# Late banks of sums, folds that wait for company, and a traded place: one edit to a planned FNet-and-attention kernel

## The chip, the cores and the metric

The kernel runs on one core of one Trainium2 chip. The metric is the device time of one execution in microseconds (us); smaller is better. The core has a matrix engine, TensorE (PE, with its weight loads shown apart as PEld), VectorE (DVE), ScalarE (ACT), GpSimd (POOL) and SyncE (SP), which here does nothing but issue transfers (DMAs). Each engine works through its own list of instructions in order; semaphores make one wait for another. TensorE writes into PSUM, which is used here as eight banks of 128 x 512 float32.

## The reference, cut to what matters

Two independent sublayers on 2048 tokens of width 448 are computed in float32 and laid side by side in the output (2048 x 896).

```
# A: FNet mixing
a = einsum("bsd,ed->bse", x, dft_hid_re);  b = einsum("bsd,ed->bse", x, dft_hid_im)
y = einsum("ts,bse->bte", dft_seq_re, a) - einsum("ts,bse->bte", dft_seq_im, b)
# B: full softmax attention, 16 heads of 28
qkv = x @ wqkv;  scores = q @ k.T * 28 ** -0.5;  p = softmax(scores, axis=-1)
out = concat_heads(p @ v) @ wo
concatenate([A, B], axis=-1)
```

The inputs of B are scaled up by 8 each, so the scores are large and the maximum has to be taken off before the exponential.

## The kernel before, in words

**Precision.** Most products run in TensorE's fast float32 form (F32R, one pass). An operand is split into a high part (`hi`) and the rest (`lo`), and hi*hi, lo*hi and hi*lo are summed: three products in place of one. Two kinds of product use plain float32 instead: probabilities times V (L736, "PV") and the fold of its partial sums (L878). Both work in column strips of the array that are 32 wide (128*32 in the profile), all others on 128 columns except a small transpose (L718).

**Stage work ("fill").** Q, K, V projections (`project`, `values`, L548), part A's hidden transforms (`hidden`, L548) and its sequence transforms (`sequence`, L663: 1536 products of 448 columns). Each takes its weights as pieces (`Piece`): a DMA into `wraw`, a cast on ACT (`whi`, L517), a subtraction on POOL (`wlo`, L523), three places of each. Fill accumulates in two PSUM banks of its own.

**Attention.** A head's 2048 queries are four chunks of 512; a unit is one chunk of one head, 64 in all, in two lanes.
- A *kept* unit (44; `unit_kept`) makes 16 score products with keys in rows (L809). ACT copies each to SBUF (L416; two score tiles share a place of the pool `kept`, a "pair"), while DVE keeps the running maximum over the tiles in `rm` (L816, L819). Then DVE turns `rm` into one maximum per query, copied to all partitions: transpose (L824), reduce (L826), three small copies (L831), a reduce over those (L836), two small copies (L834), transpose back (L842); ACT copies the result to `mb` (L844). POOL (or DVE, reading the bank) takes it off each pair (L859), ACT takes the exponential (L863), and two groups of eight PV products follow (`pv_group`).
- A *twice* unit (20; `unit_twice`) makes its scores twice: once with queries in rows (L755; DVE reduces the maximum, L759), and, after the maximum has gone through DRAM into two more rows of q, once with keys in rows (L787), which ACT exponentiates straight out of the bank (L791); then PV.

Each unit's PV accumulates in one bank `po`, copied to a place of `ou` (`unit_out`). When all units of a head are through, `out_of` folds them (L878) and sends sums and quotients through DRAM. The output projection (L988) closes the program.

**What sets the order.** Nothing is ordered by hand. `Schedule` plays the engines forward with planned costs and emits, for each engine, the ready task with the smallest key (a due time); a task that needs a place (a bank, a pair, a place of `q` or `ou`) takes it when it is emitted and gives it back when its last user is done. The planner knows that a change of TensorE between the two kinds of float costs time (`PE_TURN`): once in float32 it first looks for another float32 task (`mode` 1). `units`' due times come from `T_ATT`, `T_END` and the `ahead` factors, those of fill from `T_FILL`. The lists that come out are fixed; on the chip each engine follows its list.

**Places before.** Six banks for attention; 19 pairs in `kept`; 4 places of `q`; 5 of `ou`.

Of the kernel before, what the change touches and what calls it, by code (L numbers as in the profile page):

```python
# [24 lines left out]
P = 128  # L25
# [7 lines left out]
NKEPT = 19  # L33
# [32 lines left out]
PE_TURN = 0.33  # L66

# [99 lines left out]
class Task:  # L167
    __slots__ = ("engs", "key", "emit", "lat", "use", "lock", "left", "then", "mode", "n", "dmas", "own", "since")


class Schedule:
# [11 lines left out]
    def add(self, engs, key, emit, deps=(), acq=(), use=(), lat=0.15, lock=(), mode=0, dmas=(), own=0.0):  # L183
        t = Task()
        t.own = own
# [20 lines left out]
    def run(self):  # L206
# [10 lines left out]
        while True:  # L217
            for e in self.ENGINES:
# [8 lines left out]
                while heap:  # L227
# [8 lines left out]
                    if t.since > before or any(not p.can_take(w, before, now) for p, w in wants.items()) or any(  # L236
                            x.lock > now + 1e-9 for x in t.lock):
                        aside.append(item)
                        continue
# [79 lines left out]
def tile_kernel(ctx, tc, xa, wre, wim, wd, xb, wqkv, wo, out):  # L319
# [33 lines left out]
    q_s = new("q", [P, CH], F32R, 4, True)  # L353
# [3 lines left out]
    ou_s = new("ou", [P, CH], F32, 5, True)  # L357
# [63 lines left out]
    T_ATT, T_END, T_FILL, T_OUT = 34.0, 1100.0, 1130.0, 1100.0  # L421
# [6 lines left out]
    for lane, per, ahead, part in ((lane_r, P_R, 1.08, 1.0), (lane_k, P_K, 2.0, 1.0)):  # L428
# [220 lines left out]
    def sequence(part, made):  # L649
        src = wim if part else wre  # L650
        for tt in range(NT):
# [3 lines left out]
            for q in range(4):  # L655
                key = fkey(12, M448)
                w = Piece(lambda tt=tt, q=q: src[tt, :, q * 4:q * 4 + 4, :], key - 12)
# [86 lines left out]
    def unit_twice(u):  # L744
# [34 lines left out]
        for g in range(NT // GV):  # L779
            tiles, es = [], []  # L780
            for kt in range(GV * g, GV * (g + 1)):
                o = bank_s.slot()
                if kt % 2 == 0:
# [5 lines left out]
                    deps=[ld, before.get("rb")], use=[o, p.pair, q, KT[h][kt // 4], po])  # L789
# [6 lines left out]
    def unit_kept(u):  # L796
# [29 lines left out]
        r = dve(key, lambda o=o: nc.vector.tensor_reduce(  # L826
# [3 lines left out]
        def beside(i):  # L830
            return lambda: nc.vector.tensor_copy(pm.t[:32, i * NT:(i + 1) * NT], pm.t[32 * i:32 * i + 32, :NT])  # L831

        def back(n, o=o):
            return lambda: nc.vector.tensor_copy(o.t[n:2 * n, :NT], o.t[:n, :NT])  # L834
        r = [dve(key, beside(i), SMALL, deps=[r], use=[pm]) for i in (1, 2, 3)]
        r = dve(key, lambda o=o: nc.vector.tensor_reduce(  # L836
            o.t[:32, :NT], pm.t[:32, :4 * NT].rearrange("p (i j) -> p j i", i=4), axis=AX.X, op=ALU.min), 0.25,
            deps=r, use=[pm, o])
        for n in (32, 64):
            r = dve(key, back(n), SMALL, deps=[r], use=[o])  # L840

        t = dve(key, lambda o=o: nc.vector.transpose(pm.t, o.t[:, :NT].unsqueeze(2).to_broadcast([P, NT, 32])), 0.64,  # L842
                deps=[r], use=[pm, o])
# [25 lines left out]
    def out_of(us, rd):  # L869
# [9 lines left out]
        m = pe(key, emit, d=0.86, deps=[ou_done[u] for u in us], use=[o, *(OU[u] for u in us)], mode=1)  # L879
# [154 lines left out]
```

## Time and profile before

| | before |
|---|---|
| median of 3 runs | 1154.09 us (1153.95 to 1154.94) |
| the profiled execution's own time | 1154.71 us |
| its span, first to last instruction | 1152.5 us |
| busy: PE / PEld | 1140.0 (99%) / 780.5 (68%) us |
| busy: DVE / ACT / POOL | 988.2 (86%) / 1028.2 (89%) / 905.0 (79%) us |
| mean granted TensorE clock | 0.997 |
| PV products L736, records | 1960 + 88, mean 601 and 594 ns |

How to read it: matmuls are pipelined, so one is listed with some 0.37 to 0.41 us though the next starts 0.2 us later. What a stretch of TensorE costs is therefore read from start to start in the timeline, not from the listed durations. A float32 product shows as two records. In the timeline, rows are "start, length, engine, line, operation, out<-in", instructions of one group merged (x8), with idle time in brackets.

### The profile page before, as it was taken

What the parts mean: (1) busy time and instruction counts of PE and PEld (TensorE: products, weight loads), DVE (VectorE), ACT (ScalarE), POOL (GpSimd) and SP (SyncE); (2) the same over time, 40 slices, a digit from 0 to 9 for tenths busy, and PEclk for the clock granted to TensorE, in tenths of its full rate; (3) what the DMA queues carried; (4) which work ended last, traced back from release to release, by engine and by line L of the source; (5) the groups of instructions that cost most, each with busy time, mean ns of one, the idle gap of its engine ahead of it and who ended that gap; (6) DMA issues with size and microseconds to landing.
All of it is one profiled execution on the core that took longest, in us unless ns stands there. A gap on an engine that the chain in (4) does not pass through costs nothing.

```text
span 1152.5 us, 19482 instructions
## 1 busy us (share of the span) xinstructions
PE 1140.0 (99%) x6110; PEld 780.5 (68%) x6110; DVE 988.2 (86%) x1767; ACT 1028.2 (89%) x1765; POOL 905.0 (79%) x540
## 2 busy tenths in 40 slices
PE   8999999999999999999999999999999999999998
PEld 6976566566676667766767766666666767757577
DVE  6599988899898999999999989989899888899812
ACT  5269999899998999989999999999999899899952
POOL 3038688799798998988988899987998789596660
PEclk9999999899999999999999999999999999999999
DMA  9984344132323232232323232232333333323543
GB/s 266 186 197 144 115 163 131 44 86 76 101 86 101 83 91 68 86 105 91 108 79 102 77 115 67 84 105 96 106 96 94 94 94 105 114 64 95 157 153 122
DMA packets 111880, 125.18 MB, mean 109 GB/s; under 512 B 49369, under 2 KB 63353, under 8 KB 111777
## 3 DMA queue, kind: packets, MB, share of 16 engines
q1 hardware_dynamic: 111776, 123.94, 35.9%
q8 instruction: 48, 0.79, 0.3%
q14 instruction: 56, 0.45, 0.1%
HBM read 90.00 MB, written 33.77 MB: 107 GB/s over the span
## 4 chain that ended last, share of the span: by engine, by line
PE 86%; DVE 6%; ACT 3%; issue 2%; DMA 1%; SPq 0%; DVEq 0%; ACTq 0%
PE bank L663 25%; PE bank L736 19%; PE bank L809 13%; PE bank L548 12%; PE bank L755 6%; PE bank L787 6%; PE bank L988 3%; DVE rm L819 3%; ACT kept L416 1%; PE bank L878 1%; ACT kept L791 1%; DVE mx L759 1%; DMA kept<-wqkv 1%; DMA kept<-xb 1%; ACT kept L863 0%
## 5 line engine op out<-in xcount | busy, mean ns | idle before, releaser
L859 POOL TENSOR_TENSOR kept<-kept,mb 128x1024 f32<-128x1024 f32 x259 | 617.3, 2407 | 68.1 <-ACT mb L844 54.5
L819 DVE TENSOR_TENSOR rm<-bank,rm 128x512 f32<-128x512 f32 x616 | 421.9, 685 | 57.2 <-ACT kept L416 20.9
L416 ACT ACTIVATE kept<-bank 128x512 f32<-128x512 f32 (+1 forms) x673 | 390.9, 642 | 54.0 <-PE bank L809 34.2
L863 ACT ACTIVATE kept<-kept 128x1024 f32<-128x1024 f32 x343 | 370.6, 1118 | 7.8 <-POOL kept L859 5.6
L663 PE MATMUL bank<-big,whi 128*128 128x448 f32 x1024 | 325.8, 368 | 0.0
L523 POOL TENSOR_TENSOR wlo<-wraw,whi 128x512 fp32r<-128x512 f32 (+1 forms) x166 | 204.7, 1236 | 129.2 <-ACT whi L517 71.2
L809 PE MATMUL bank<-q,k 84*128 84x512 f32 x704 | 270.6, 410 | 3.3 <-DVE bank L842 1.4
L736 PE MATMUL bank<-kept,v 128*32 128x512 f32 x1960 | 242.0, 601 | 0.3 <-DVE rm L819 0.3
L759 DVE TENSOR_REDUCE mx<-bank 128x1 f32<-128x512 f32 x320 | 216.3, 681 | 11.1 <-PE bank L755 8.6
L663 PEld LDWEIGHTS bank<-big,whi 128*128 128x128 f32 x1024 | 193.9, 190 | 30.2 <-issue 4.2
L791 ACT ACTIVATE kept<-bank 128x512 f32<-128x512 f32 x294 | 184.1, 650 | 7.6 <-PE bank L787 7.5
L663 PE MATMUL bank<-big,wlo 128*128 128x448 f32 x512 | 188.2, 368 | 0.0
L809 PEld LDWEIGHTS bank<-q,k 84*128 84x128 f32 x704 | 129.4, 188 | 76.1 <-DVE rm L819 11.6
L736 PEld LDWEIGHTS bank<-kept,v 128*32 128x32 f32 x1960 | 56.6, 110 | 123.6 <-issue 112.9
L755 PE MATMUL bank<-k,q 84*128 84x512 f32 x320 | 130.4, 414 | 0.5 <-DVE mx L759 0.2
L787 PE MATMUL bank<-q,k 86*128 86x512 f32 x320 | 127.9, 410 | 0.1
L517 ACT ACTIVATE whi<-wraw 128x512 fp32r<-128x512 f32 x167 | 115.4, 691 | 5.9 <-DMA wraw<-wqkv 2.5
L663 PEld LDWEIGHTS bank<-big,wlo 128*128 128x128 f32 x512 | 97.1, 190 | 12.4
L859 DVE TENSOR_TENSOR kept<-kept,bank 128x1024 f32<-128x1024 f32 x84 | 100.9, 1210 | 4.6 <-ACT mb L844 4.6
L787 PEld LDWEIGHTS bank<-q,k 86*128 86x128 f32 x320 | 59.8, 189 | 35.3 <-issue 6.7
L755 PEld LDWEIGHTS bank<-k,q 84*128 84x128 f32 x320 | 60.3, 189 | 33.7 <-DVE rm L819 8.3
L548 PE MATMUL bank<-wd,whi 128*128 128x448 f32 x256 | 79.2, 368 | 0.1
(82 smaller groups left out, 1065.0 us busy)
## 6 DMA issues: line engine op xcount, KB each, us to landing
wraw<-wre SPq DMA_DIRECT2D x64, 256.0 KB
wraw<-wim SPq DMA_DIRECT2D x64, 256.0 KB
qkd<-wd SPq DMA_DIRECT2D x32, 256.0 KB
wraw<-xa SPq DMA_DIRECT2D x32, 256.0 KB
k<-qkd SPq DMA_DIRECT2D x64, 112.0 KB
q<-qkd SPq DMA_DIRECT2D x64, 112.0 KB
out<-kept SPq DMA_DIRECT2D x31, 224.0 KB
qkd<-kept SPq DMA_DIRECT2D x24, 256.0 KB
```

Of the source, the lines that this page charges most:

```text
L416: nc.scalar.activation(dst, src, AF.Copy)
L523: b = sch.add(e, at, lambda g: eng[g].tensor_tensor(self.lo.t[:, :n], raw.t[:, :n], f32(self.hi.t)[:, :n], op=ALU.subtract), deps=[a], acq ...
L548: nc.tensor.matmul(o.t[:, :cols], w(), x(), start=(i == 0), stop=(i == n - 1))
L663: nc.tensor.matmul(o.t[:, :D], a.t[:, k, :], b[:, q * 4 + k, :], start=(q == 0 and k == 0 and j == 0), stop=(q == 3 and k == 3 and j == 2))
L736: nc.tensor.matmul(o.t[j * VW:(j + 1) * VW, :], VT[h].t[:, kt // 4, j, :], pairs[i // 2].t[:, i % 2, :], start=(kt < 4), stop=(kt >= NT - 4))
L755: m = pe(key, lambda e, o=o, kc=kc, qt=qt: nc.tensor.matmul(o.t, q.t[:KR, qt * P:(qt + 1) * P], KT[h][kc].t[:KR, :], start=True, stop=True ...
L759: ms.append(dve(key - 20, lambda o=o, kc=kc, qt=qt: nc.vector.tensor_reduce(mx.t[:, qt, kc:kc + 1], o.t, axis=AX.X, op=ALU.max), deps=[m], ...
L787: m = pe(key, lambda e, o=o, kt=kt: nc.tensor.matmul(o.t, KT[h][kt // 4].t[:KR + 2, kt % 4 * P:(kt % 4 + 1) * P], q.t[:KR + 2, :], start=T ...
L809: m = pe(key, lambda e, o=o, kt=kt: nc.tensor.matmul(o.t, KT[h][kt // 4].t[:KR, kt % 4 * P:(kt % 4 + 1) * P], q.t[:KR, :], start=True, sto ...
L819: prev = dve(key - 20, lambda o=o: nc.vector.tensor_tensor(rm.t, o.t, rm.t, op=ALU.max), deps=[m, prev], use=[rm, o], lock=[o], own=RAW)
L859: eng[e].tensor_tensor(s.t, s.t, over_pair(pm.t if e == "DVE" else mb.t), op=ALU.add)
L863: es.append(act(key, lambda s=s: nc.scalar.activation(s.t, s.t, AF.Exp, scale=SCALE), 0.96, deps=[sh], use=[s]))
```

## The change

It does six things, all through the planner's inputs.

1. *Banks of sums late.* In `unit_twice` the 16 second score products no longer use `po`, so the bank is taken by the first PV group and not by the first second score.
2. *First bank of the maxima.* In `unit_kept` the bank that the first transpose fills is given back after the reduce. The small copies and the small reduce now stay inside the second bank (columns 64 to 80), and the transpose back writes a third.
3. *Folds wait.* A fold that is ready while TensorE is in the fast form is put off until a PV group is ready too, or 15 planned us have passed (`JOIN`), or nothing else is ready; not in the last 30 us of attention.
4. *Places.* `kept` 20 pairs in place of 19, paid with one place of `q` (4 to 3) and one of `ou` (5 to 4).
5. *Keys.* `T_END`, `T_OUT` 1100 to 1104, `T_FILL` 1130 to 1132; `ahead` 1.08 to 1.07 and 2.0 to 2.06.
6. *Pieces* of `sequence` are due one planned us earlier.

No product is added or taken away.

```diff
-NKEPT = 19
+NKEPT = 20
+JOIN = 15.0
...
+                    if e == "PE" and mode == 0 and t.wait and now - t.since < t.wait and not any(
+                            y[2].mode == 1 and y[2].n not in done for y in heap):
+                        first = first or item
+                        aside.append(item)
+                        continue
...
-    q_s = new("q", [P, CH], F32R, 4, True)
+    q_s = new("q", [P, CH], F32R, 3, True)
-    ou_s = new("ou", [P, CH], F32, 5, True)
+    ou_s = new("ou", [P, CH], F32, 4, True)
...
-    T_ATT, T_END, T_FILL, T_OUT = 34.0, 1100.0, 1130.0, 1100.0
+    T_ATT, T_END, T_FILL, T_OUT = 34.0, 1104.0, 1132.0, 1104.0
-    for lane, per, ahead, part in ((lane_r, P_R, 1.08, 1.0), (lane_k, P_K, 2.0, 1.0)):
+    for lane, per, ahead, part in ((lane_r, P_R, 1.07, 1.0), (lane_k, P_K, 2.06, 1.0)):
...
-                w = Piece(lambda tt=tt, q=q: src[tt, :, q * 4:q * 4 + 4, :], key - 12)
+                w = Piece(lambda tt=tt, q=q: src[tt, :, q * 4:q * 4 + 4, :], key - 13)
...
-                    deps=[ld, before.get("rb")], use=[o, p.pair, q, KT[h][kt // 4], po])
+                    deps=[ld, before.get("rb")], use=[o, p.pair, q, KT[h][kt // 4]])
...
-            return lambda: nc.vector.tensor_copy(o.t[n:2 * n, :NT], o.t[:n, :NT])
+            return lambda: nc.vector.tensor_copy(pm.t[n:2 * n, 4 * NT:5 * NT], pm.t[:n, 4 * NT:5 * NT])
...
-        t = dve(key, lambda o=o: nc.vector.transpose(pm.t, o.t[:, :NT].unsqueeze(2).to_broadcast([P, NT, 32])), 0.64,
-                deps=[r], use=[pm, o])
+        p1, pm = pm, bank_s.slot()
+        t = dve(key, lambda pm=pm: nc.vector.transpose(pm.t, p1.t[:, 4 * NT:5 * NT].unsqueeze(2).to_broadcast([P, NT, 32])), 0.64,
+                deps=[r], use=[pm, p1])
...
-        m = pe(key, emit, d=0.86, deps=[ou_done[u] for u in us], use=[o, *(OU[u] for u in us)], mode=1)
+        m = pe(key, emit, d=0.86, deps=[ou_done[u] for u in us], use=[o, *(OU[u] for u in us)], mode=1,
+               wait=JOIN if key < T_END - 30 else 0.0)
```

The whole list of every engine is reordered, from the first attention units on. Three places follow. Line numbers of the changed kernel are 6 to 8 higher: L736 is L742, L755 L761, L787 L793, L809 L815, L859 L866, L878 L885, L988 L996.

TensorE, the last fold of a head with four units in both programs (`ou` are its four units' sums, `fold` the constant that adds them). Before:

```order
L718 MATMUL bank_231<-ident,nm_220 4x128
L809 MATMUL bank_226<-q_188,k_184 128x512
L809 MATMUL bank_228<-q_188,k_184 128x512
L809 MATMUL bank_230<-q_188,k_184 128x512
L663 MATMUL bank_224<-big,whi_173 128x448
L878 MATMUL bank_227<-ou_215,fold 32x512
L878 MATMUL bank_227<-ou_216,fold 32x512
L878 MATMUL bank_227<-ou_214,fold 32x512
L878 MATMUL bank_227<-ou_213,fold 32x512
L809 MATMUL bank_231<-q_188,k_184 128x512
```

Now:

```order
L742 MATMUL bank_227<-kept_209,v_186 32x512 x2
L742 MATMUL bank_226<-kept_208,v_186 32x512 x2
L742 MATMUL bank_226<-kept_203,v_186 32x512 x2
L742 MATMUL bank_226<-kept_192,v_186 32x512 x2
L742 MATMUL bank_226<-kept_205,v_186 32x512 x2
L885 MATMUL bank_230<-ou_213,fold 32x512
L885 MATMUL bank_230<-ou_215,fold 32x512
L885 MATMUL bank_230<-ou_214,fold 32x512
L885 MATMUL bank_230<-ou_216,fold 32x512
L815 MATMUL bank_228<-q_190,k_185 128x512
```

The fold stood alone between fast products; it now stands behind two PV groups.

DVE, the maxima of the last kept unit (banks by their numbers). Before:

```order
L824 STREAM_TRANSPOSE bank4_228<-rm0_211 128x512
L826 TENSOR_REDUCE bank3_227<-bank4_228 128x16
L831 COPY bank3_227<-bank3_227 32x16 x3
L836 TENSOR_REDUCE bank4_228<-bank3_227 32x16
L834 COPY bank4_228<-bank4_228 32x16
L834 COPY bank4_228<-bank4_228 64x16
L842 STREAM_TRANSPOSE bank3_227<-bank4_228 128x512
```

Now:

```order
L830 STREAM_TRANSPOSE bank7_230<-rm0_211 128x512
L832 TENSOR_REDUCE bank4_227<-bank7_230 128x16
L837 COPY bank4_227<-bank4_227 32x16 x3
L842 TENSOR_REDUCE bank4_227<-bank4_227 32x16
L840 COPY bank4_227<-bank4_227 32x16
L840 COPY bank4_227<-bank4_227 64x16
L849 STREAM_TRANSPOSE bank2_225<-bank4_227 128x512
```

The first bank was in use over all seven rows; it is now in use over two.

TensorE in part A's first hidden transform, ahead of the two PV groups that stand between its third piece of weights (`whi_172`) and its fourth. Before:

```order
L548 MATMUL bank_225<-wd,whi_172 128x448 x2
L809 MATMUL bank_229<-q_191,k_183 128x512
L809 MATMUL bank_226<-q_191,k_183 128x512
L809 MATMUL bank_230<-q_191,k_183 128x512
L755 MATMUL bank_228<-k_180,q_189 128x512
L809 MATMUL bank_231<-q_191,k_183 128x512
L755 MATMUL bank_228<-k_180,q_189 128x512
L755 MATMUL bank_227<-k_180,q_189 128x512
L755 MATMUL bank_228<-k_180,q_189 128x512
L736 MATMUL bank_229<-kept_202,v_187 32x512 x2
```

Now:

```order
L554 MATMUL bank_224<-wd,whi_172 128x448
L761 MATMUL bank_225<-k_180,q_190 128x512
L793 MATMUL bank_229<-q_189,k_180 128x512
L554 MATMUL bank_224<-wd,wlo_175 128x448
L761 MATMUL bank_228<-k_182,q_190 128x512
L554 MATMUL bank_224<-wd,whi_172 128x448 x2
L793 MATMUL bank_230<-q_189,k_180 128x512
L742 MATMUL bank_227<-kept_209,v_187 32x512 x2
```

Before, the third piece was used up and eight score products stood there without fill among them; now products with the third piece stand between the scores up to the PV groups (one more follows behind them).

More of the change, by code (lines that the diff above doesn't have):

```diff
@@ L167 @@
 class Task:
-    __slots__ = ("engs", "key", "emit", "lat", "use", "lock", "left", "then", "mode", "n", "dmas", "own", "since")
+    __slots__ = ("engs", "key", "emit", "lat", "use", "lock", "left", "then", "mode", "n", "dmas", "own", "since", "wait")
 class Schedule:
@@ L181, in __init__, with add @@
         self.now = 0.0
-    def add(self, engs, key, emit, deps=(), acq=(), use=(), lat=0.15, lock=(), mode=0, dmas=(), own=0.0):
+    def add(self, engs, key, emit, deps=(), acq=(), use=(), lat=0.15, lock=(), mode=0, dmas=(), own=0.0, wait=0.0):
         t = Task()
-        t.own = own
+        t.own, t.wait = own, wait
         t.engs, t.key, t.emit, t.lat, t.lock, t.mode = engs, key, emit, lat, lock, mode
@@ L825, in unit_kept, with back @@
         pm = bank_s.slot()
-        r = dve(key, lambda o=o: nc.vector.tensor_reduce(
+        r = dve(key, lambda o=o, pm=pm: nc.vector.tensor_reduce(
             pm.t[:, :NT], o.t.rearrange("p (j r) -> p j r", r=32), axis=AX.X, op=ALU.max, negate=True), deps=[t], use=[o, pm], own=RAW_S)
         def beside(i):
-            return lambda: nc.vector.tensor_copy(pm.t[:32, i * NT:(i + 1) * NT], pm.t[32 * i:32 * i + 32, :NT])
-        def back(n, o=o):
-            return lambda: nc.vector.tensor_copy(o.t[n:2 * n, :NT], o.t[:n, :NT])
+            return lambda pm=pm: nc.vector.tensor_copy(pm.t[:32, i * NT:(i + 1) * NT], pm.t[32 * i:32 * i + 32, :NT])
+        def back(n, pm=pm):
+            return lambda: nc.vector.tensor_copy(pm.t[n:2 * n, 4 * NT:5 * NT], pm.t[:n, 4 * NT:5 * NT])
         r = [dve(key, beside(i), SMALL, deps=[r], use=[pm]) for i in (1, 2, 3)]
-        r = dve(key, lambda o=o: nc.vector.tensor_reduce(
-            o.t[:32, :NT], pm.t[:32, :4 * NT].rearrange("p (i j) -> p j i", i=4), axis=AX.X, op=ALU.min), 0.25,
-            deps=r, use=[pm, o])
+        r = dve(key, lambda p1=pm: nc.vector.tensor_reduce(
+            p1.t[:32, 4 * NT:5 * NT], p1.t[:32, :4 * NT].rearrange("p (i j) -> p j i", i=4), axis=AX.X, op=ALU.min), 0.25,
+            deps=r, use=[pm])
         for n in (32, 64):
-            r = dve(key, back(n), SMALL, deps=[r], use=[o])
-        t = dve(key, lambda o=o: nc.vector.transpose(pm.t, o.t[:, :NT].unsqueeze(2).to_broadcast([P, NT, 32])), 0.64,
-                deps=[r], use=[pm, o])
+            r = dve(key, back(n), SMALL, deps=[r], use=[pm])
+        p1, pm = pm, bank_s.slot()
+        t = dve(key, lambda pm=pm: nc.vector.transpose(pm.t, p1.t[:, 4 * NT:5 * NT].unsqueeze(2).to_broadcast([P, NT, 32])), 0.64,
+                deps=[r], use=[pm, p1])
         ld = act(key, lambda: nc.scalar.activation(mb.t, pm.t, AF.Copy), deps=[t], use=[pm, mb], lock=[pm])
```

## The prediction

> **What bounds the kernel now.** I read the page first (busy time, the forty slices, the chain that ended last), then the timeline of TensorE start to start, then the windows around its gaps.
>
> ```profile
> PE 1140.0 (99%) x6110; PEld 780.5 (68%) x6110; DVE 988.2 (86%) x1767; ACT 1028.2 (89%) x1765; POOL 905.0 (79%) x540
> PE   8999999999999999999999999999999999999998
> PE 86%; DVE 6%; ACT 3%; issue 2%; DMA 1%; SPq 0%; DVEq 0%; ACTq 0%
> ```
>
> TensorE has work in every slice and the chain runs through it for 86%. So the end moves by what leaves TensorE's list, and by the stalls in it; what the other four engines gain or lose counts only where TensorE waits. All 6110 records are products that the change keeps. What can change is the cost of going between the two kinds of product, and the stalls.
>
> **The price of a turn.** A visit to the float32 products, one PV group, then a visit of two groups, then a fold alone:
>
> ```profile
> 403.61 0.39 PE L809 MATMUL bank<-q,k 84*128 84x512 f32 x1
> 403.84 0.37 PE L663 MATMUL bank<-big,whi 128*128 128x448 f32 x1
> 404.05 0.37 PE L663 MATMUL bank<-big,wlo 128*128 128x448 f32 x1
> ...
> 405.29 0.39 PE L755 MATMUL bank<-k,q 84*128 84x512 f32 x1
> 405.61 1.06 PE L736 MATMUL bank<-kept,v 128*32 128x512 f32 x8
> ...
> 407.46 0.73 PE L787 MATMUL bank<-q,k 86*128 86x512 f32 x2
> 408.04 0.37 PE L663 MATMUL bank<-big,whi 128*128 128x448 f32 x1
> ```
>
> ```profile
> 398.43 0.62 PE L736 MATMUL bank<-lent,v 128*32 128x512 f32 x2
> ...
> 402.00 0.73 PE L809 MATMUL bank<-q,k 84*128 84x512 f32 x2
> ```
>
> ```profile
> 223.18 0.36 PE L548 MATMUL bank<-wd,whi 128*128 128x448 f32 x1
> 223.47 1.07 PE L878 MATMUL bank<-ou,fold 128*32 128x512 f32 x8
> 224.47 0.51 PE L809 MATMUL bank<-q,k 84*128 84x512 f32 x1
> 224.81 0.40 PE L787 MATMUL bank<-q,k 86*128 86x512 f32 x1
> ```
>
> An ordinary score product takes 403.84 - 403.61 = 0.23 us from start to start, one of 448 columns 404.05 - 403.84 = 0.21. More closely, the 66 products of the last row but one quoted below take (13.66 - 0.37) / 65 = 0.205, and 512/448 of that is 0.235 for the scores. Three losses make up a turn. Going in: 405.61 - 405.29 = 0.32 where 0.235 is usual, 0.09 lost (the fold: 0.29 for 0.205, the same). Coming out: two groups in one visit take 402.00 - 398.43 = 3.57, one takes 407.46 - 405.61 = 1.85; so a group is worth 1.72 and 0.13 is lost. Then the first fast product behind it: two took 408.04 - 407.46 = 0.58 for 0.47, 0.11 lost (behind the fold 0.34 for 0.235, 0.10). The sum is **0.33 us a turn**, whatever stands in the visit.
>
> **The change, part by part.**
>
> *Turns.* Counting visits over the two lists of TensorE: 111 before, 97 now. Folds that make a visit alone fall from 7 to 2, which is the waiting fold's work (3 of the change). Visits with PV fall from 104 to 95 for the same 128 groups: visits of a single group from 83 to 66, of two from 18 to 25, of three from 3 to 4. That comes from the replanning as a whole. 14 x 0.33 = **4.6 us** off a list that has no cover of its own: it goes off the end unless a stall takes it back.
>
> *The largest stall.* TensorE's longest gap after the start-up is the place of the third order piece.
>
> ```profile
> 202.99 0.39 PE L809 MATMUL bank<-q,k 84*128 84x512 f32 x1
> 203.94 1.10 PE L809 MATMUL bank<-q,k 84*128 84x512 f32 x2 [0.56 <-DVE rm L819]
> 206.26 0.79 PE L809 MATMUL bank<-q,k 84*128 84x512 f32 x1 [0.63 <-DVE rm L819]
> 209.16 1.08 PE L736 MATMUL bank<-kept,v 128*32 128x512 f32 x4
> ```
>
> ```profile
> 203.80 0.68 DVE L759 TENSOR_REDUCE mx<-bank 128x1 f32<-128x512 f32 x1
> 204.40 0.68 DVE L819 TENSOR_TENSOR rm<-bank,rm 128x512 f32<-128x512 f32 x1
> ...
> 193.04 14.19 POOL L859 TENSOR_TENSOR kept<-kept,mb 128x1024 f32<-128x1024 f32 x6
> 207.18 1.01 POOL L523 TENSOR_TENSOR wlo<-wraw,whi 128x384 fp32r<-128x384 f32 x1
> ```
>
> ```profile
> 180.00:202.00 22.00, 22.00 (x123) 14.70 (x122) 20.65 (x38) 21.40 (x38) 18.91 (x13) 1.00 0.44 140
> 202.00:210.00 8.00, 6.44 (x18) 2.73 (x20) 7.71 (x14) 7.87 (x14) 7.36 (x6) 0.74 0.10 28
> ```
>
> ```profile
> 209.23 5.36 PE bank L736 x32
> 398.50 3.57 PE bank L736 x32
> ```
>
> POOL subtracts six pairs in a row (14.19 us) and the next `wlo` is ready only at 208.2. Out of fill, TensorE has eight score products, each of which needs a bank that DVE empties at 0.60 us apiece (204.40 - 203.80). From 202.99 to 209.16 they take 6.17 us; eight at 0.235 are 1.88 and the turn's 0.09 belongs to the turn: 4.2 lost. In the same window the granted clock (the third number from the end) is 0.74, 1.00 in the window ahead, and the two PV groups behind take 5.36 where two take 3.57 at 398.50: 1.8 more. So this stall is worth **6.0 us**. The Trainium skill (TensorE: Matmul & The Clock Gate, Part 1) says that the clock is halved once a window of 3.4 us sees too little activity. By that rule any stall that trips it costs half a window, 1.7 us, on top of itself, which the 1.8 us above bears out; the no-change rival below would then end at 1155.4.
>
> In the new list the eight products in a row are gone, with fill between the scores up to the PV groups. But the run of six subtractions on POOL is still there between the third and the fourth piece, so I can't exclude that TensorE runs dry in front of the fourth. Bounds: 6.0 us gained, or nothing. I take half, **3.0 us**.
>
> *Banks.* The late `po` leaves one of six banks free while the first eight second scores of each of 20 units go through; the early return of the first bank spares it from the reduce to the end of the transpose back:
>
> ```profile
> 74.56 0.60 DVE L831 COPY bank<-bank 32x16 f32<-32x16 f32 x3
> 75.19 0.22 DVE L836 TENSOR_REDUCE bank<-bank 32x16 f32<-32x64 f32 x1
> 75.88 0.73 DVE L842 STREAM_TRANSPOSE bank<-bank 128x512 f32<-128x512 f32 x1
> ...
> 75.52 0.40 PE L548 MATMUL bank<-big,wlo 128*128 128x512 f32 x1
> 76.66 1.08 PE L809 MATMUL bank<-q,k 84*128 84x512 f32 x2 [0.74 <-DVE bank L842]
> ...
> PE bank L809 <- DVE bank L842: 1.4, 2, 0.7
> ```
>
> Here TensorE waited for just that bank; the preceding product started at 75.52, so 0.90 us was lost (76.66 - 75.52 - 0.235). A third bank is now wanted for the transpose back, so a wait there can be new too. By this row the 44 units could gain up to 0.90 each at a place like this, but TensorE's waits on L842 are 2 in all (1.4 us), so the bounds are 1.4 gained and, with a new wait as long at two places, 1.4 lost. I take nothing: the planner has already spent the spare banks on the denser order counted above. The small reduce now reads and writes one bank; the copies L831 do that in 0.20 each, the reduce took 0.22 between two banks. Even at twice that, 44 x 0.22 = 10 us lie in DVE's idle 164.
>
> *Work that changes engine.* In the lists DVE has 15 more copies of banks (65 to 80, 0.60 us each) and 4 fewer subtractions of a pair (85 to 81), ACT 15 fewer copies, POOL 4 more subtractions (2.4 us each). DVE gains some 4 us of work and POOL 10, under 164 and 248 us idle. The cover is gone only in stretches like the one at 203.
>
> *One place of `q` less.* This is the edit that speaks against the change. I added up TensorE's products, at their distances above, between the last one that reads a place of `q` and the first of the place's next unit. Before: 24 us in the median, under 6 us in 3 cases of 60. Now: 7.0 us in the median, under 6 us in 19 of 61, never under 5.0. A new load must fit into that.
>
> ```profile
> 36.05 0.46 SPq L690 DMA_DIRECT2D q<-qkd  x1
> 36.56 0.42 SPq L691 DMA_DIRECT2D q<-qkd  x1
> ...
> 40.32 0.40 PE L755 MATMUL bank<-k,q 84*128 84x512 f32 x1
> ```
>
> The two transfers of a load were issued from 36.05 and the product that reads them started at 40.32 without a wait: at most 4.27 us. The last reader's length, 0.4, comes ahead of it. That makes 4.7 against 5.0, so a load fits where SP is free, by the loosest bound. SP isn't always free:
>
> ```profile
> SPq L516 <- POOL wlo L523: 160.0, 81, 10.3
> ```
>
> SP takes its list in order, and stands 81 times, up to 10.3 us, in front of a load of weights whose place POOL hasn't freed; a load of `q` behind it waits as well, and behind that TensorE's next score, and everything in its list. Bounds: nothing, or a microsecond in each of the 19 cases, 19 us. I take **1.0 us**, since the planned order knows of SP's waits and the surplus is only what the plan has wrong. [...]
>
> *The end.* The keys put attention's end later against fill. The last fold's results must come back before the last 44 products:
>
> ```profile
> 1135.23 13.66 PE L988 MATMUL bank<-wd,k 128*128 128x448 f32 x66
> 1135.27 1.55 DVE L412 TENSOR_TENSOR k<-kept,k 128x256 fp32r<-128x256 f32 x4
> ```
>
> The last chunk's products begin 22 x 0.205 behind 1135.23, at 1139.7; their operands were ready at 1136.8: 2.9 us to spare. In the new list, TensorE has 27.1 us of work between the last fold and those products, where the old list has 28.2. So 1.8 us are left: nothing lost; if the chain were 3 us slower, 1.2 us would be.
>
> *Start.* TensorE's list is the same over its first 73 rows, into the first score products, so the start-up gaps stay.
>
> **The sum.** 1152.5 - 4.6 - 3.0 + 1.0 = 1145.9 us of span. The median of the runs lies 1.6 above the profiled span (1154.09; the profiled execution itself took 1154.71, 2.2 above). So **1147.5 us**, 0.57% less.
>
> **Rivals.**
>
> *Slower: loads of q late.* One mechanism: SP stands behind a weight load, the load of q is issued late, and TensorE's list stops at that unit's first score. For it: 19 gaps under 6 us where there were 3. Against: 4.7 us is the loosest bound. From 0.40 us in each of the 19 cases it eats the 7.6 of both gains, from 0.52 the kernel is slower by 0.2%; at 0.6 the time is 1154.1 - 4.6 - 3.0 + 11.4 = 1157.9. Chance 0.11.
>
> *No change: the stalls move.* TensorE runs dry in front of the fourth piece as before (the 3.0 is not gained) and one stall more of the size of the one at 203, without the clock's share (4.2), appears: 1154.1 - 4.6 + 4.2 = 1153.7. For it: DVE and ACT are at 86 and 89%, and a reordered list meets new places. Chance 0.16.
>
> *Faster than I say.* All of the stall at 203 goes and q costs nothing: 1154.1 - 4.6 - 6.0 = 1143.5; with the waits on L842 too, 1142.1. Chance 0.15.
>
> *The change does nothing that it says* is excluded by the lists: 97 visits are 97.
>
> **Chances and range.** My forecast, turns gained and stalls no worse, has 0.58. A measurement of this kernel tells about 0.2% from no change, 2.3 us: faster is below 1151.8, slower above 1156.4. The forecast (0.58, all but 0.03 of it below 1151.8) and the faster rival (0.15) make 0.70 for faster; of the no-change rival 0.13 and the 0.03 give 0.16 for the same; the late loads and 0.03 of the moved stalls, 0.14 for slower. The range 1142 to 1154 takes in the faster rival's end and all of the no-change rival's point, and leaves out the slower one and a tail; the forecast's own range is 1144.5 to 1150.5.
>
> **What would show it.** Right: two-group visits more often, 14 fewer turns at the same 0.33; at about 195 to 215 us no half clock, and L736 x32 at 3.57; no wait of TensorE behind L690 or L691. Wrong: gaps in front of a unit's first score with a load of q as the releaser; a window with the clock under 1.00; a stall of TensorE in front of the fourth hidden piece; or turns that cost other than 0.33 when the groups stand closer.

## The result and the profile after

The changed kernel takes 1146.94 us (median of 6, 1145.6 to 1149.28), the kernel before, beside it, 1155.2 us (median of 6, 1153.95 to 1156.85): a ratio of 0.993, 95% interval 0.9917 to 0.9943. The forecast was 1147.5. The profiled execution of the changed kernel took 1145.6, the fastest of its six; its span is 1143.7. What the traces below split up is one execution of each kernel, and executions of one list differ (the six here by 3.7 us), so a term of a microsecond or two is not sure.

The same lines of the page as before, now of the changed kernel (busy time of each engine; TensorE's slices; shares of the chain that ended last):

```profile
PE 1133.0 (99%) x6110; PEld 782.5 (68%) x6110; DVE 988.6 (86%) x1777; ACT 1024.7 (90%) x1750; POOL 914.5 (80%) x545
PE   9999999999999999999999999999999999999998
PE 90%; DVE 4%; ACT 3%; issue 2%; DMA 1%; SPq 0%; DVEq 0%; ACTq 0%
```

TensorE has the same 6110 records and the chain now runs through it for 90% instead of 86%. Line numbers have moved: L736, L809, L819, L842 and L859 of the kernel before are L742, L815, L825, L849 and L866 now. Where the 8.7 us of span went is read from the distances of TensorE's starts. In every trace I added them up: each product at the distance that its form has inside its own kind (0.205 or 0.235, a PV group 1.717, a fold 0.859), each visit to the float32 products at 0.33, and the rest is called stalls. The products alone come to 1088.1 us in every list here (42 small transposes are in that; with their median distances it would be some 2 us less, and the stalls of every row 2 us more, alike), the first product starts at 1.4, and what lies behind the last start is called the end.

| kernel | median | span | visits | turns | stalls before 30 us | stalls behind 30 us | end |
|---|---|---|---|---|---|---|---|
| before | 1155.2 | 1152.5 | 111 | 36.7 | 5.2 | 17.1 | 4.0 |
| after | 1146.9 | 1143.7 | 97 | 32.1 | 4.0 | 13.9 | 4.2 |

Turns give 4.6, stalls behind 30 us 3.2, stalls before 30 us 1.2, the end takes 0.3 back: 8.7 us of span. The 1.2 before 30 us is no part of the change: the list of TensorE is the same there, and over the nine traces of whole kernels (these two and the seven below without added products) this term lies between 4.0 and 5.9. It can be seen on one product that both lists have at the same place, before and now:

```profile
30.05 0.39 PE L548 MATMUL bank<-big,wlo 128*128 128x512 f32 x1
```

```profile
28.83 0.39 PE L554 MATMUL bank<-big,wlo 128*128 128x512 f32 x1
```

The 3.2 hides two large terms of opposite sign. The stall at 203 us is gone. Windows of the changed kernel, the first the one that the prediction shows of the kernel before (stretch, its length, then busy time of PE, PEld, DVE, ACT, POOL, then the granted clock, share of DMA, GB/s):

```profile
202.00:210.00 8.00, 8.00 (x53) 4.36 (x52) 7.69 (x18) 8.00 (x14) 7.19 (x6) 1.00 0.20 53
...
1055.00:1063.00 8.00, 7.70 (x49) 4.05 (x37) 8.00 (x11) 8.00 (x13) 7.86 (x7) 1.00 0.39 123
1063.00:1071.00 8.00, 6.61 (x29) 3.81 (x31) 7.31 (x12) 8.00 (x14) 4.15 (x4) 0.79 0.39 131
```

TensorE's timeline at the first of them (start, duration, engine, line), then POOL's:

```profile
205.09 0.57 PE L554 MATMUL bank<-wd,whi 128*128 128x448 f32 x2
205.50 0.40 PE L793 MATMUL bank<-q,k 86*128 86x512 f32 x1
205.83 3.64 PE L742 MATMUL bank<-kept,v 128*32 128x512 f32 x32
209.41 0.74 PE L815 MATMUL bank<-q,k 84*128 84x512 f32 x2
```

```profile
194.43 11.87 POOL L866 TENSOR_TENSOR kept<-kept,mb 128x1024 f32<-128x1024 f32 x5
206.26 1.01 POOL L529 TENSOR_TENSOR wlo<-wraw,whi 128x384 fp32r<-128x384 f32 x1
```

TensorE is busy for all of the 8 us where it had 6.44, the clock is 1.00 where it was 0.74, and the 32 records of PV take 209.41 - 205.83 = 3.58 where they took 5.36. POOL still has a run of subtractions (five in 11.87 us; it was six in 14.19), and the next `wlo` is only 1 us earlier. What changed is what TensorE has until then: fill up to 205.5, and behind it two PV groups that start 3.3 us earlier than they did. They cover the wait for `wlo`.

In its place there is a new stall, near the end of attention. TensorE's timeline, then DVE's ahead of it:

```profile
1062.33 0.36 PE L669 MATMUL bank<-big,wlo 128*128 128x448 f32 x1
1063.67 0.50 PE L815 MATMUL bank<-q,k 84*128 84x512 f32 x1 [0.97 <-DVE rm L825]
1064.80 0.50 PE L793 MATMUL bank<-q,k 86*128 86x512 f32 x1 [0.63 <-DVE kept L866]
1065.40 0.79 PE L815 MATMUL bank<-q,k 84*128 84x512 f32 x1
1065.98 0.57 PE L669 MATMUL bank<-big,whi 128*128 128x448 f32 x1
```

```profile
1053.69 1.21 DVE L866 TENSOR_TENSOR kept<-kept,bank 128x1024 f32<-128x1024 f32 x1
1054.82 0.69 DVE L825 TENSOR_TENSOR rm<-bank,rm 128x512 f32<-128x512 f32 x1
1055.42 1.21 DVE L866 TENSOR_TENSOR kept<-kept,bank 128x1024 f32<-128x1024 f32 x1
```

DVE has subtractions of the last units (L866) between its maxima (L825): by these rows a score bank comes free every 1055.42 - 1053.69 = 1.73 us, where maxima alone free one in 0.60. By the windows above DVE is busy 8.00 of 8 from 1055 to 1063; then scores wait for banks, the clock falls to 0.79 (a window with the clock under 1.00 was one of the prediction's signs of being wrong), and in all 4.5 us are lost between 1060 and 1070. So the stalls behind 30 us are -5.9 at 203, +4.5 at 1063 and -1.8 in all the other places.

### The profile page after: what moved, and what is told of

Same layout as the page of the kernel before. It is cut to its first block, busy times and chain, and to the rows that moved or that the text cites. A ratio compares the mean times of both kernels' runs of the same rounds, so it can differ in the third digit from the quotient of the medians.

```text
span 1143.7 us, 19466 instructions
## 1 busy us (share of the span) xinstructions
PE 1133.0 (99%) x6110; PEld 782.5 (68%) x6110; DVE 988.6 (86%) x1777; ACT 1024.7 (90%) x1750; POOL 914.5 (80%) x545
## 4 chain that ended last, share of the span: by engine, by line
PE 90%; DVE 4%; ACT 3%; issue 2%; DMA 1%; SPq 0%; DVEq 0%; ACTq 0%
PE bank L669 26%; PE bank L742 19%; PE bank L815 14%; PE bank L554 13%; PE bank L761 7%; PE bank L793 6%; PE bank L996 3%; PE bank L885 1%; DVE rm L825 1%; ACT kept L422 1%; ACT kept L797 1%; ACT kept L870 1%; DMA kept<-wqkv 1%; DMA kept<-xb 0%; DVE mx L765 0%
## 5 line engine op out<-in xcount | busy, mean ns | idle before, releaser
L866 POOL TENSOR_TENSOR kept<-kept,mb 128x1024 f32<-128x1024 f32 x259 | 619.0, 2413 | 73.4 <-ACT mb L851 65.4
L825 DVE TENSOR_TENSOR rm<-bank,rm 128x512 f32<-128x512 f32 x616 | 421.5, 684 | 43.2 <-ACT kept L422 13.4
L870 ACT ACTIVATE kept<-kept 128x1024 f32<-128x1024 f32 x340 | 369.5, 1130 | 8.6 <-POOL kept L866 4.6
L529 POOL TENSOR_TENSOR wlo<-wraw,whi 128x512 fp32r<-128x512 f32 (+1 forms) x166 | 205.5, 1241 | 105.1 <-ACT whi L523 76.4
L815 PE MATMUL bank<-q,k 84*128 84x512 f32 x704 | 266.3, 411 | 2.5 <-DVE rm L825 1.3
L742 PE MATMUL bank<-kept,v 128*32 128x512 f32 x1960 | 240.5, 596 | 0.0
L797 ACT ACTIVATE kept<-bank 128x512 f32<-128x512 f32 x300 | 192.6, 671 | 4.2 <-PE bank L793 4.1
L815 PEld LDWEIGHTS bank<-q,k 84*128 84x128 f32 x704 | 129.5, 188 | 79.3 <-DVE rm L825 19.3
L742 PEld LDWEIGHTS bank<-kept,v 128*32 128x32 f32 x1960 | 57.8, 109 | 123.8 <-issue 107.0
L793 PE MATMUL bank<-q,k 86*128 86x512 f32 x320 | 128.1, 406 | 1.0 <-DVE kept L866 0.6
L761 PE MATMUL bank<-k,q 84*128 84x512 f32 x320 | 127.8, 407 | 0.3 <-ACT kept L870 0.2
L866 DVE TENSOR_TENSOR kept<-kept,bank 128x1024 f32<-128x1024 f32 x81 | 97.6, 1211 | 5.9 <-ACT mb L851 5.4
L761 PEld LDWEIGHTS bank<-k,q 84*128 84x128 f32 x320 | 60.0, 188 | 30.8 <-DVE rm L825 4.1
L793 PEld LDWEIGHTS bank<-q,k 86*128 86x128 f32 x320 | 60.2, 189 | 24.5 <-DVE rm L825 5.3
```

Of the source, the lines that this page charges most:

```text
L529: b = sch.add(e, at, lambda g: eng[g].tensor_tensor(self.lo.t[:, :n], raw.t[:, :n], f32(self.hi.t)[:, :n], op=ALU.subtract), deps=[a], acq ...
L742: nc.tensor.matmul(o.t[j * VW:(j + 1) * VW, :], VT[h].t[:, kt // 4, j, :], pairs[i // 2].t[:, i % 2, :], start=(kt < 4), stop=(kt >= NT - 4))
L761: m = pe(key, lambda e, o=o, kc=kc, qt=qt: nc.tensor.matmul(o.t, q.t[:KR, qt * P:(qt + 1) * P], KT[h][kc].t[:KR, :], start=True, stop=True ...
L793: m = pe(key, lambda e, o=o, kt=kt: nc.tensor.matmul(o.t, KT[h][kt // 4].t[:KR + 2, kt % 4 * P:(kt % 4 + 1) * P], q.t[:KR + 2, :], start=T ...
L815: m = pe(key, lambda e, o=o, kt=kt: nc.tensor.matmul(o.t, KT[h][kt // 4].t[:KR, kt % 4 * P:(kt % 4 + 1) * P], q.t[:KR, :], start=True, sto ...
L825: prev = dve(key - 20, lambda o=o: nc.vector.tensor_tensor(rm.t, o.t, rm.t, op=ALU.max), deps=[m, prev], use=[rm, o], lock=[o], own=RAW)
```

## Experiments

Ratios are to the kernel before, run on the same chip, with 95% intervals. The five kernels of the next part were run once each and have no interval.

### What a turn costs

The prediction read 0.33 us a turn out of neighbouring starts. Here turns are put in. In the middle of each of the 128 PV groups, behind the fourth of its eight products, stand two more. They add zeros to the group's bank, so the sums stay what they are. `identr` is the constant `ident` held as a float32r tile; the columns 96 to 99 of its first 96 rows are zeros.

```diff
...
                                  start=(kt < 4), stop=(kt >= NT - 4))
+                if i == 3:
+                    for _ in range(2):
+                        nc.tensor.matmul(o.t[:, :4], identr[:96, :], identr[:96, 96:100], start=False, stop=False)
```

The other four have another line in the place of the last: float32 over 128 columns (`ident[:96, :]` and `ident[:96, 96:100]`), fast in a strip of 32 (`o.t[:VW, :4]`, `identr[:96, :VW]`), float32 in a strip (the same of `ident`), and fast with 448 columns, one column of zeros read 448 times.

The fast pair over 128 columns:

> The changed kernel with two small fast products (96 rows, 128 columns of a constant, 4 columns of zeros, added to the bank) put into the middle of each of the 128 PV groups: 128 visits more, 225 in all, and 256 small products; the result of each sum is unchanged. Theory (a change there and back costs 0.33 us whatever stands between): 1146.9 + 128 x 0.33 = 1189 us, and the 256 products' own length on top, as the control with the same products of the groups' own kind has it. Rival (what I read as a turn belongs to the score products' operands, not to the change of kind): no more than the control, and 0.1 us or less between a group's halves beside the products.

The float32 pair over 128 columns:

> The same place, two small float32 products over 128 columns of the constant. Theory K (the price belongs to the change between float32 and fast products): no turn, so the control's time. Theory S (it belongs to the change between strips of 32 columns and the full 128): 128 x 0.33 = 42 us above the control, as much as the fast pair.

The fast pair in a strip:

> The same place, two small fast products over a strip of 32 columns. Theory K (change between float32 and fast): 42 us above the control. Theory S (change between strip and full width): the control's time.

The control, float32 in a strip:

> The control: the same place, two small float32 products over a strip of 32 columns, the groups' own kind. Both theories: no turn, 97 visits; 1146.9 us and the 256 products' own length, which the trace gives as the distance of their starts (by the length of a whole strip product, 0.21 us for 512 columns, at most 256 x 0.21 = 55 us).

The fast pair of 448 columns:

> As the fast pair in the middle of each PV group, but the two fast products have 448 columns (all zeros), whose distance of starts the rows give as 0.205 us. Theory (a turn costs 0.33 us, 0.10 of it at the second fast product): a visit of a single group takes 1.854 + 0.33 + 2 x 0.205 = 2.59 us, the whole 1146.9 + 128 x 0.74 = 1241.6 us. Rival (0.19 us, what the pair of 4 columns shows in its steps out and back in, without a loss at the second product): 2.45 us a visit, 1223 us.

Times: 1195.89, 1226.18, 1177.16, 1157.01 and 1230.97 us. In the times, part of the added work is hidden in stalls that were there anyway, so the visits tell more. For the visits of one PV group that stand complete in the trace (55 in each), the medians of the distances between starts, in ns. A group has four sets of records, four strips each, that start 7 apart; the row of a set gives the distance from its last record to what comes next. The pair stands between the second set and the third:

| | whole visit | set 1 | set 2 | inside the pair | pair to set 3 | set 3 | set 4, to the score or fill behind |
|---|---|---|---|---|---|---|---|
| after, no pair | 1854 | 433 | 409 | | | 409 | 523 |
| fast, 128 columns | 2305 | 433 | 522 | 133 | 181 | 433 | 522 |
| float32, 128 columns | 2530 | 433 | 523 | 132, 112, 112 | 182 | 433 | 523 |
| fast, strip | 2145 | 433 | 522 | 53 | 101 | 433 | 522 |
| float32, strip | 1963 | 433 | 409 | the pair's records run among the third set's | | | 523 |
| fast, 448 columns | 2570 | 434 | 522 | 293 | 285 | 433 | 522 |

(A float32 product has two records, so a float32 pair has four.)

One visit of the last of these kernels as its timeline shows it (L745 are the strips of PV, L749 the pair):

```profile
408.56 0.36 PE L672 MATMUL bank<-big,whi 128*128 128x448 f32 x1
408.85 1.07 PE L745 MATMUL bank<-kept,v 128*32 128x512 f32 x8
409.85 0.65 PE L749 MATMUL bank<-ident 96*128 96x448 f32 x2
410.43 1.06 PE L745 MATMUL bank<-kept,v 128*32 128x512 f32 x8
411.43 0.50 PE L821 MATMUL bank<-q,k 84*128 84x512 f32 x1
```

The pair of 448 columns makes a visit 0.716 us longer. Two such products are worth 0.410; **0.306 us** is the turn put in. Its parts stand in the steps: out 522 - 409 = 0.113, and 0.024 in the first set behind the return (433 for 409); 293 - 205 = 0.088 at the second fast product; 285 - 205 = 0.080 going back in. That is the 0.13, 0.10 and 0.09 of the prediction, 8% smaller in sum, and near the theory's 2.59 us (2.57), not the rival's 2.45. The time of the whole, 1230.97, is 10.6 under the theory's 1241.6: 128 x 0.716 = 91.6 us were added and 84.0 appeared (85.4 by the spans, 1229.1 for 1143.7). So the stalls became some 6 us shorter; that the other engines used the longer time to catch up is likely, and not shown.

Of the theories on what makes the turn, neither K nor S holds. The strip pair changes only the kind, the wide float32 pair only the width, and both pay the same 0.11 out and 0.02 behind the return as the pair that changes both; the control, which changes neither, pays nothing (409 behind its second set). So a visit ends wherever the next product differs in kind or in width. The Trainium skill (TensorEngine Tiling (Array Packing), Key Properties) says that a change of the tiling mode drains TensorE. The wide float32 pair agrees, at 0.114 us lost, though no run here shows the draining itself; the fast strip pair pays as much without a change of width.

### One part undone

Each of the next three is the changed kernel with one part taken back. The order is planned anew each time.

```diff
-                    deps=[ld, before.get("rb")], use=[o, p.pair, q, KT[h][kt // 4]])
+                    deps=[ld, before.get("rb")], use=[o, p.pair, q, KT[h][kt // 4], po])
```

> The changed kernel with the accumulation bank of a kind-two unit held again from its first second score on; all else as changed. The replanned list has 94 visits to the float32 products (97 in the changed kernel). Theory (turns and stalls set the end): 3 turns less, 1.0 us, stalls of some 18 us as in the changed kernel, so 1145.9 us, give or take 4 for stalls that move. Rival (the freed bank is what gained): up to 0.90 us lost in each of the 20 units that now run with five banks, so 1150 us or more, with waits of TensorE on banks as the stalls that grew.

```diff
-JOIN = 15.0
+JOIN = 0.0
```

> The changed kernel with the folds' wait set to nothing (JOIN 0); all else as changed. The list has 102 visits, 9 of them folds alone (97 and 2 in the changed kernel). Theory (0.33 us a turn): 5 turns more, 1.65 us, so 1148.6 us, and the trace shows 0.33 for each visit. Rival (the stall at 203 us was what gained, and turns cost nothing that counts): 1146.9 us, and if the stall comes back with this list, 1152.9.

```diff
-NKEPT = 20
+NKEPT = 19
...
-    q_s = new("q", [P, CH], F32R, 3, True)
+    q_s = new("q", [P, CH], F32R, 4, True)
...
-    ou_s = new("ou", [P, CH], F32, 4, True)
+    ou_s = new("ou", [P, CH], F32, 5, True)
```

> The changed kernel with the old places: 19 pairs, 4 for q, 5 for the sums (changed: 20, 3, 4). The list has 97 visits, as many as the changed kernel's. Theory (a load of q fits into the shorter gap, so the fourth place is worth nothing): 1146.9 us, give or take 4 for stalls that move; no wait on a q load in either. Rival (the third place costs 1.0 us or more): 1146 us or less, with small gaps at the first scores gone. A second rival (the twentieth pair is what carries the change): 1150 or more.

| kernel | median | ratio | span | visits | turns | stalls before 30 us | behind 30 us | end |
|---|---|---|---|---|---|---|---|---|
| late bank undone | 1163.07 | 1.0073 (1.006 to 1.0085) | 1161.3 | 94 | 31.1 | 4.6 | 31.8 | 4.2 |
| fold's wait undone | 1157.01 | 1.0017 (1.0008 to 1.0026) | 1154.0 | 102 | 33.8 | 4.3 | 22.4 | 3.9 |
| places undone | 1161.71 | 1.0055 (1.0041 to 1.0069) | 1161.9 | 97 | 32.1 | 5.9 | 30.4 | 3.9 |

My theory failed in all three, and for one reason: the turns moved as counted, and the stalls did not stay near 14 us but went to 22 to 32. The kernel with fewer turns than the change (94) is the slowest, slower than before. The late bank's rival, 1150 or more, gave the right side; so did the second rival of the places. (The profiled execution with the places undone is the slowest of its five, 2.3 us over their median.)

Two of these stalls, to see what they are. The late bank undone (the wait on a score bank that the transpose back L849 holds), then the fold's wait undone (fill waits for its bank, which DVE's L596 empties, behind maxima in DVE's list):

```profile
687.95 0.72 PE L815 MATMUL bank<-q,k 84*128 84x512 f32 x2
690.21 1.39 PE L815 MATMUL bank<-q,k 84*128 84x512 f32 x3 [1.55 <-DVE bank L849]
```

```profile
176.79 1.30 PE L761 MATMUL bank<-k,q 84*128 84x512 f32 x3
180.57 1.22 PE L554 MATMUL bank<-big,whi 128*128 128x512 f32 x2 [2.48 <-DVE kept L596]
```

The waits of the kept units' scores (L815) on L849, as the view of waits sums them (total us, times, longest), of the changed kernel and then of the one with the late bank undone. PEld is the weight load, which runs ahead of its product:

```profile
PEld bank L815 <- DVE bank L849: 3.6, 6, 1.1
PE bank L815 <- DVE bank L849: 0.2, 1, 0.2
```

```profile
PEld bank L815 <- DVE bank L849: 7.8, 14, 2.0
PE bank L815 <- DVE bank L849: 2.4, 3, 1.5
```

With the bank held early, more and longer waits for just such a bank stand in the trace. That is where a scarce bank would show, but it is 6.4 us of waits more (10.2 for 3.8), some of them covered, against 17.9 us of stalls that came. The rest stands at many places with DVE's maxima or ACT's copies as releasers. So the question became what any new order costs.

### Another order for no reason of the change

```diff
-RAW = 0.19
+RAW = 0.179
```

> The changed kernel with a planner's constant moved a little that belongs to no part of the change (RAW, the time from one instruction to the next on an engine that reads what it wrote, 0.179 for 0.19): the work is the same, the order is another one, with 91 visits, the fewest of a handful of such lists (97 in the changed kernel). Theory (turns set the end, stalls stay some 18 us): 6 turns less, 2.0 us, 1144.9 us. Rival (each new order brings stalls of its own, and the kept lists are the good ones): 1150 us or more, with single stalls of one to four us at other places, as in the runs that undid one part. Then a part's loss by its undoing holds that price of any new order too.

It took 1155.78 us, ratio 1.0009 (1.0 to 1.0019): 91 visits, turns 30.1, stalls 5.3 before 30 us and **28.3 behind**, end 3.9 (span of the profiled run 1157.1; it is the slowest of the ten, 3.2 us over their median). Its largest stall, TensorE above and DVE below:

```profile
1071.76 0.50 PE L815 MATMUL bank<-q,k 84*128 84x512 f32 x1 [0.39 <-DVE rm L825]
1073.48 1.10 PE L815 MATMUL bank<-q,k 84*128 84x512 f32 x2 [1.23 <-DVE rm L825]
1074.68 0.58 PE L793 MATMUL bank<-q,k 86*128 86x512 f32 x1
1076.41 0.80 PE L815 MATMUL bank<-q,k 84*128 84x512 f32 x1 [1.15 <-DVE rm L825]
```

```profile
1071.62 1.21 DVE L866 TENSOR_TENSOR kept<-kept,bank 128x1024 f32<-128x1024 f32 x1
1072.75 0.68 DVE L825 TENSOR_TENSOR rm<-bank,rm 128x512 f32<-128x512 f32 x1
1073.35 0.68 DVE L424 COPY ou<-bank 128x512 f32<-128x512 f32 x1
```

It is the place and the make of the changed kernel's stall at 1063, 7.2 us of it here. The rival is right: a kernel with all parts of the change, six turns fewer, and no other work, is as slow as the kernel before. So 8.8 us of the loss in each undoing (16.1, 10.1 and 14.8 us over the changed kernel) may be the price of an order for which the constants were not tuned. One such order was run, picked for its few turns, so the typical price is not known, and how much of the 16.1 and the 14.8 belongs to the bank and to the places **stays open**.

### Two parts alone

The other direction is the kernel before, with its own constants, and two parts of the change. These constants are not tuned for the new order either, so what it gains is gained in spite of that, or by luck of the order.

```diff
-NKEPT = 19
+NKEPT = 20
...
-    q_s = new("q", [P, CH], F32R, 4, True)
+    q_s = new("q", [P, CH], F32R, 3, True)
...
-    ou_s = new("ou", [P, CH], F32, 5, True)
+    ou_s = new("ou", [P, CH], F32, 4, True)
...
-                    deps=[ld, before.get("rb")], use=[o, p.pair, q, KT[h][kt // 4], po])
+                    deps=[ld, before.get("rb")], use=[o, p.pair, q, KT[h][kt // 4]])
```

> The kernel before with two parts of the change alone: the sum's bank taken late, and the places 20 pairs, 3 of q, 4 of sums; no waiting folds, no early first bank, the old due times. The list has 102 visits, 8 of them folds alone. Theory (these two carry the stalls' gain, since undoing either cost 15 us): turns -3.0 and the stalls some 4 us less, 1147.5 us, with the stall at 203 us gone. Rival (as predicted, banks count nothing, only turns): 1154.6 - 3.0 = 1151.6 us. Second rival (only the whole, tuned together, is fast): 1155 us or more.

It took 1149.29 us, ratio 0.9954 (0.9936 to 0.9972): 5.9 us of the change's 8.3. Turns 33.8, stalls 5.3 before 30 us and 14.7 behind, end 3.9. It lies between the theory's 1147.5 and the first rival's 1151.6; the turns are the 3.0 of both, and the stalls behind 30 us are 2.4 less, a little over half of what the theory gave. Two things stand in this list. The visits with PV fall from 104 to 94 (folds alone are 8 where they were 7), so the closer grouping of PV can come without the waiting fold, the early first bank and the new due times. That the two parts are what causes it is not shown: the moved constant alone took 97 visits to 91. And the stall at 203 is gone:

```profile
196.00:204.00 8.00, 8.00 (x39) 6.63 (x36) 8.00 (x15) 7.97 (x16) 7.84 (x5) 1.00 0.36 124
204.00:215.00 11.00, 10.97 (x64) 6.91 (x65) 10.76 (x21) 11.00 (x20) 5.42 (x7) 1.00 0.19 49
```

But it is gone from every new order. From 202 to 210 us TensorE is busy for 8.00 of 8 in all eight traces of other lists (the change, the three with one part undone, the moved constant, this one and the two below), where the kernel before has 6.44. With the late bank undone, then with the constant moved:

```profile
202.00:210.00 8.00, 8.00 (x38) 5.76 (x40) 7.90 (x14) 8.00 (x16) 7.34 (x5) 1.00 0.20 57
```

```profile
202.00:210.00 8.00, 8.00 (x40) 6.36 (x42) 7.78 (x14) 8.00 (x16) 7.25 (x6) 1.00 0.28 89
```

So that stall belonged to the old order, and no part of the change is shown to have removed it. A part of the 2.4 here may be luck of the order as well.

### The new stall at 1063 us

```diff
-LATE = 110.0
+LATE = 95.0
```

> The changed kernel with LATE 95 instead of 110: the subtractions of one more of the last units (the one that begins at 998 us by the plan) may go to POOL alone, so the six that stand between the maxima on DVE at 1053 to 1065 us go away from there. 98 visits. Theory (the stall of 4.5 us at 1063 comes from DVE, which then empties a score bank in 1.73 us in place of 0.60): that stall goes, a turn is added, 1146.9 - 4.5 + 0.3 = 1142.7 us. Rival (POOL becomes late in its place, the PV groups wait for their pairs): the stall stays or moves by a few us, 1146 to 1150.

It took 1146.11 us, ratio 0.9923 (0.9911 to 0.9936), against 0.993 of the change: no difference that can be told. Its windows, DVE's row where the subtractions stand, and TensorE's where another stall is:

```profile
1055.00:1063.00 8.00, 8.00 (x51) 3.97 (x50) 8.00 (x10) 8.00 (x14) 7.71 (x5) 1.00 0.29 89
1063.00:1071.00 8.00, 7.91 (x40) 5.08 (x42) 7.10 (x15) 8.00 (x15) 4.65 (x4) 1.00 0.50 158
```

```profile
1053.70 4.60 DVE L866 TENSOR_TENSOR kept<-kept,bank 128x1024 f32<-128x1024 f32 x4
```

```profile
1045.57 0.47 PE L669 MATMUL bank<-big,wlo 128*128 128x448 f32 x1 [1.13 <-POOL wlo L529]
```

The stall is gone from 1063 (PE 7.91 of 8, clock 1.00), as the theory had it, but not for its reason: six subtractions still stand on DVE between 1053 and 1063, four of them now in a row and two between maxima. DVE has four fewer in its list (77 for 81), and those stood elsewhere, at 1033 to 1039. And the rival came too: POOL, with more to do, delivers a `wlo` late at 1045.57. In all 2.7 us are lost from 1040 to 1070 instead of 4.5, a turn is added, and 1.8 us of stalls behind 30 us are gained in the traces. That DVE's interleaving makes the stall is argued from the rows of three traces; it was not isolated.

### A version that beats both

```diff
-LATE = 110.0
+LATE = 95.0
...
-JOIN = 15.0
+JOIN = 30.0
...
-    T_ATT, T_END, T_FILL, T_OUT = 34.0, 1104.0, 1132.0, 1104.0
+    T_ATT, T_END, T_FILL, T_OUT = 33.0, 1102, 1132.0, 1102
...
-    for lane, per, ahead, part in ((lane_r, P_R, 1.07, 1.0), (lane_k, P_K, 2.06, 1.0)):
+    for lane, per, ahead, part in ((lane_r, P_R, 1.06, 1.0), (lane_k, P_K, 2.03, 1.0)):
```

The constants are those, of the sets tried, for which the planner books the earliest end for its own order.

> The changed kernel with other due times, all of them constants of the planner: attention begins at 33 and ends at 1102 (34 and 1104), the second passes 1.06 and 2.03 periods behind the first (1.07, 2.06), LATE 95, JOIN 30. 94 visits. Theory (with the subtractions of the last units spread and fewer turns): 1.0 us from turns, some 4 us from the stall at 1063, so 1142 us. Rival (the stalls move to other places): 1147 us or more.

It took 1142.11 us (1140.43 to 1142.91), ratio 0.989 (0.9875 to 0.9906). Span 1140.9: turns 31.1 (1.0 less than the change), stalls 5.1 before 30 us and 11.2 behind it (2.7 less), end 4.0. The chain and the window at 1063, then its one stall with a lower clock:

```profile
PE 94%; DMA 2%; DVE 2%; ACT 1%; issue 1%; SPq 0%; ACTq 0%; DVEq 0%
```

```profile
1063.00:1071.00 8.00, 8.00 (x45) 6.24 (x47) 7.14 (x16) 8.00 (x15) 3.42 (x3) 1.00 0.40 132
174.00:184.00 10.00, 8.74 (x38) 4.32 (x37) 8.09 (x19) 9.09 (x16) 9.41 (x6) 0.83 0.53 165
```

The theory's number is right and its rival's is not: the turns' gain is there and the stall at 1063 is gone. But a new stall of 3.1 us at 177 takes most of that gain back, so part of the 2.7 was gained at other places, and that the sum fits is partly luck. Several constants were moved at once; what each of them does is not separated.

## Why the prediction came out right, and where its steps did not

**Turns: right.** 97 visits stand in the trace, 14 fewer, and the price, put in from outside, is 0.31 for the 0.33 read from neighbours. 4.6 us of the gain is this term. The folds alone do fall from 7 to 2, and they are 8 and 9 in the two lists in which folds don't wait, as the prediction had it. The closer grouping of PV it gave to the replanning as a whole; nothing here shows more than that: the late bank with the new places has it without the other parts, and the order with the moved constant has still more of it for no reason of the change.

**The stall at 203: the mechanism right, the size off.** The step took half of 6.0 because the run of subtractions on POOL was still in the list. The run is still there (11.87 us) and the stall is wholly gone, 5.9 us. The step looked at what is late and not at what TensorE has meanwhile: fill to 205.5, then PV. It could not know that the stall is missing from all eight other orders, so that "half" was a choice between two bounds and not a reading.

**No stall elsewhere: wrong.** The sum held no new stall. One of 4.5 us came, at 1063, in size that of the no-change rival's "one stall more" of 4.2, though not alone: the gain at 203 came in full beside it. The step that failed is *work that changes engine*: DVE's and POOL's idle totals were taken as cover. DVE's busy time rose by 0.4 us (988.2 to 988.6) where the step had some 4, POOL's by 9.5 where it had 10; but cover is a matter of the stretch, and in the stretch 1055 to 1063 DVE has 8.00 of 8.

**Banks worth nothing, bounds of 1.4: not borne out.** The bounds came from the two rows of PE that name the transpose back, while in the kernel before its waits stand on weight loads as well:

```profile
PEld bank L809 <- DVE bank L842: 4.7, 10, 1.2
```

A wait that the load takes need not lose time, but it shows how often a bank is short: 12 times, not 2. (In the changed kernel these waits come to 3.8 us, for 6.1 before.) And the step priced the bank inside the old order, though it also changes which orders are possible. Two parts alone gave 5.9 us, 3.0 of them turns, and undoing the late bank lost 16.1, of which 8.8 or so can be the order's. That is more than 1.4 for the resources together, unless the order did it; the share of the bank alone is open.

**One place of `q` less: a loss that did not show.** The term was +1.0, with 19 us as the upper bound. In the changed kernel no wait of TensorE names a load of q from `qkd`, though 19 gaps are under 6 us; giving the fourth place back (with the other two places) made nothing faster. The loads fit, as the loosest bound of 4.7 us had it. Nothing in this trace speaks for the slower rival.

**The end and the start: right.** The end moved by 0.3. The start's list is the same; the 1.2 us by which its stalls differ is within what nine executions of that start show (4.0 to 5.9).

So 1147.5 against 1146.9 is a right sum of terms that were wrong and cancelled, and that is luck: the gain is put 2.9 too low at 203, 1.0 too low at `q` and 1.8 too low in small stalls, and 4.5 too high by leaving out the stall at 1063. The turn term carries its own weight; the stalls behind 30 us were forecast 2.0 less and are 3.2 less, but from other places. The order with the moved constant shows how easily it could have come out otherwise: with 91 turns and every part of the change, stalls alone brought the time back to 1155.8.

## What to carry to other kernels

Where an order is planned, a change of resources is priced by two sums over the trace: the turns that it saves, which can be counted in the list beforehand, and the stalls, which belong to the order and not to the part. A part that is undone without tuning the constants again measures the part and a new order together; run at least one order that differs for no reason before such a loss is believed, and do the part alone on the old kernel as well. A stall that is gone is put down to a part only if other orders still have it. A stall is covered or not by what the waiting engine has left to do at that moment, so read a stretch of 8 us, not the engine's idle total.

## What the hardware showed that was not expected

Leaving a float32 strip product costs TensorE 0.11 us before the next product, and 0.02 more in the first set behind the return, whether the next one differs only in kind (fast in a strip) or only in width (float32 over 128 columns); a product of the same kind and width costs none of it. And with TensorE's work made 91.6 us longer by the pair of 448 columns, the kernel became 84.0 us slower in one run: about 8% of the added work went into stalls that were there.
